# Attention of the first two batches: PE transposes in place of DMA transposes, small copies on GpSimd, key tiles with a pitch of 144

## The chip, the cores and the metric

One core of a Trainium2 chip runs the whole kernel. The metric is the device time of one execution in microseconds (us), taken as the median of several runs. TensorE is called PE, VectorE DVE, ScalarE ACT, GpSimd POOL or GpSimd, SyncE SP. SP issues DMAs only; ACT and GpSimd issue a few as well.

## The reference

Attention with RMS-normed queries and keys, followed by an MLP with a hard-swish-like activation. All inputs are float32.

```
q, k, v: (B=8, H=12, S=448, D=64);  g_q, g_k: (64,)
q_n = q / sqrt(mean(q*q, -1) + 1e-6) * g_q          # k_n the same with g_k
attn = softmax(q_n @ k_n.T / sqrt(64));  x = attn @ v
x -> (B*S = 3584, H*D = 768)
h = x @ w_in (768, 2048);  g = h * clip(h + 3, 0, 6) / 6;  out = g @ w_out (2048, 768)
```

## The kernel before

Heads go in pairs: a pair P is two heads of one batch, six pairs to a batch, 48 in all. A head has 448 rows; the first 384 ("main", three tiles of 128) are handled per pair, the last 64 ("rest") per two batches, so that two batches fill 128 partitions.

For a pair, q and k are loaded into `qk` (L145), squared (L136 on ACT for pairs under 4, L138 on GpSimd for the others), summed by DVE (L166), turned into 1/rms by ACT (L130, L131), and scaled to bf16 in `qks` by GpSimd (L178). v is cast into `va` by GpSimd (L188), which also builds `vbd`, the rest's v masked by head (L215). A DMA transpose issued by SP (`trans_pair`, L257) brings `qks` into `kq`, where keys and queries lie with the head dimension on the partitions. `pad_pair` then has DVE copy the 64 rest columns of q from `rT` into `kq` (L266) and write the keys twice into `kp`, each time multiplied by a column of `gmask` that is zero for one head of the two and holds the gains for the other (L269). The rest's q and k go the same way for two batches at once: scaled into `qkrs` (L233), transposed by DMA into `rT` (`trans_rest`, L240), padded into `kbd` by DVE (`pad_rest`, L248).

Scores are seven matmuls a pair into PSUM, 128 keys by 448 queries (L285); ACT takes the exponential of each (L286). `av` multiplies them with v into `x_ps` (L294, L297); DVE divides (L311, L313) into `xn`, and a DMA transpose (`xtrans`, L349) puts it into `xT`. The x of the rest goes over `xr` and `xrT`, from where DVE copies it into `xT` (L358).

The MLP of batch G reads `xT`: `h_part` (matmul L369, ACT L374, DVE L376 into `gT`) and `y_part` (matmul L388, DVE L394, store). `h` of batch b-1 and `y` of batch b-2 are merged into the attention of batch b by estimated cost, so batch 0 has no MLP beside it and batch 1 has `h` alone. The weights are loaded by GpSimd's DMA queue, w_in with pairs 3 to 9, w_out with pairs 11 to 14.

PSUM has three banks for scores, one each for `x_ps` and `r_ps`, and three (`ps_M`) for h and y. Pools set how far loads run ahead: five `qk`, four `vf`, four `kq`, three `kp`. Before the main loop a prologue sets the order of all engines by hand. In the main loop the program's order binds SP and GpSimd alone; the framework orders PE, DVE and ACT by readiness. `att_items(P)` emits, in this order: loads of P+6, the rest's step, squares of P+4, `trans_pair` and `pad_pair` of P+2, scaling and cast of P+3, the scores of P+1 merged with the av of P, and `xtrans` of P one pair later.

## Time and profile before

| | |
|---|---|
| time, three runs | 532.46 us median (524.71 to 533.09) |
| the profiled execution | 534.13 us, span 532.4 us |
| PE, matmul | 438.5 us busy, 82% of the span |
| DVE | 285.9 us, 54% |
| ACT | 298.8 us, 56% |
| GpSimd | 214.0 us, 40% |
| granted PE clock, mean | 0.946 of full speed |
| bytes by DMA | 67.44 MB, 127 GB/s over the span |

Busy shares are means over a span with different stages. The clock is a share of 2.4 GHz, of which 1.2 GHz is the lower level. The profiled execution is one run of its own; the rows below are of it.

### The profile page before, as it was taken

What the parts mean: (1) busy time and instruction counts of PE and PEld (TensorE: products, weight loads), DVE (VectorE), ACT (ScalarE), POOL (GpSimd) and SP (SyncE); (2) the same over time, 40 slices, a digit from 0 to 9 for tenths busy, and PEclk for the clock granted to TensorE, in tenths of its full rate; (3) what the DMA queues carried; (4) which work ended last, traced back from release to release, by engine and by line L of the source; (5) the groups of instructions that cost most, each with busy time, mean ns of one, the idle gap of its engine ahead of it and who ended that gap; (6) DMA issues with size and microseconds to landing.
All of it is one profiled execution on the core that took longest, in us unless ns stands there. A gap on an engine that the chain in (4) does not pass through costs nothing.

```text
span 532.4 us, 9016 instructions
## 1 busy us (share of the span) xinstructions
PE 438.5 (82%) x3344; PEld 254.0 (48%) x3344; DVE 285.9 (54%) x545; ACT 298.8 (56%) x583; POOL 214.0 (40%) x247
## 2 busy tenths in 40 slices
PE   0365565769988985999889997889978999999996
PEld 0143332436444553556444554555534566665553
DVE  2686476785645736555545636465545544334421
ACT  3665735757567754566566765576646766623310
POOL 3867676573534655154334643525234410000000
PEclk9987867888999999799998998999989999999999
DMA  9899999996658375435769365446664132120012
GB/s 207 214 224 191 196 140 216 187 186 142 147 140 165 85 185 112 96 96 144 142 139 145 90 170 127 98 98 154 161 109 83 45 90 60 31 76 30 15 64 70
DMA packets 139755, 67.44 MB, mean 127 GB/s; under 512 B 90560, under 2 KB 139712, under 8 KB 139712
## 3 DMA queue, kind: packets, MB, share of 16 engines
q1 hardware_dynamic: 131904, 59.99, 51.2%
q0 software_dynamic: 5440, 6.29, 8.0%
q10 hardware_dynamic: 2368, 0.59, 0.6%
q8 instruction: 26, 0.43, 0.3%
q14 instruction: 17, 0.14, 0.1%
HBM read 45.61 MB, written 11.01 MB: 106 GB/s over the span
## 4 chain that ended last, share of the span: by engine, by line
PE 45%; DMA 18%; issue 12%; DVE 11%; POOL 8%; SPq 3%; ACT 1%; POOLq 0%
PE y_ps L388 20%; PE h_ps L369 14%; DMA kq<-qks 10%; PE s_ps L285 6%; DVE kp L269 4%; PE x_ps L294 3%; POOL sq L138 3%; DMA qkr<-in_q_dram 3%; POOL qks L178 3%; DMA rT<-qkrs 2%; DMA qk<-in_q_dram 2%; DVE xn L313 1%; SPq L145 1%; DVE kq L266 1%; DVE kbd L248 1%
## 5 line engine op out<-in xcount | busy, mean ns | idle before, releaser
L286 ACT ACTIVATE eT<-s_ps,zero_c 128x448 bf16<-128x448 f32 x336 | 202.7, 634 | 79.7 <-PE s_ps L285 78.8
L369 PE MATMUL h_ps<-xT,w_in_sb 128*128 128x384 bf16 (+1 forms) x768 | 190.4, 364 | 20.3 <-DVE gT L376 12.9
L388 PE MATMUL y_ps<-w_out_sb,gT 128*128 128x384 bf16 x896 | 177.7, 331 | 12.9 <-DVE gT L376 12.6
L285 PE MATMUL s_ps<-kq,kp 128*128 128x448 bf16 x288 | 109.1, 387 | 30.6 <-DVE kp L269 30.0
L388 PEld LDWEIGHTS <-gT 128*128 128x128 bf16 x896 | 86.0, 99 | 68.9 <-issue 17.6
L374 ACT ACTIVATE t_sb<-h_ps,half_c 128x384 f32<-128x384 f32 (+1 forms) x128 | 80.9, 632 | 57.0 <-PE h_ps L369 36.9
L369 PEld LDWEIGHTS <-w_in_sb 128*128 128x128 bf16 x768 | 73.7, 100 | 73.2 <-issue 21.9
L188 POOL CAST va<-vf 128x384 bf16<-128x384 f32 x48 | 24.5, 509 | 194.3 <-PE r_ps L297 96.1
L376 DVE SCALAR_TENSOR_TENSOR gT<-t_sb,h_ps 128x384 bf16<-128x384 f32 (+1 forms) x128 | 78.6, 615 | 42.3 <-ACT t_sb L374 41.8
L294 PEld LDWEIGHTS <-eT 128*128 128x128 bf16 x1152 | 68.4, 105 | 65.5 <-issue 31.0
L269 DVE TENSOR_SCALAR kp<-kq,gmask 128x384 bf16<-128x384 bf16 x96 | 57.2, 626 | 78.0 <-DMA kq<-qks 77.9
L178 POOL TENSOR_TENSOR qks<-qk,rs 128x384 bf16<-128x384 f32 x96 | 77.8, 831 | 19.1 <-ACT rs L131 11.9
L294 PE MATMUL x_ps<-va,eT 128*128 128x65 bf16 x864 | 59.4, 203 | 24.8 <-DVE xn L313 20.2
L138 POOL TENSOR_TENSOR sq<-qk 128x768 f32<-128x768 f32 x44 | 64.6, 1468 | 5.8 <-DMA qk<-in_q_dram 5.7
L166 DVE TENSOR_REDUCE ssq<-sq 128x12 f32<-128x768 f32 x48 | 45.4, 946 | 32.5 <-POOL sq L138 24.8
L285 PEld LDWEIGHTS <-kp 128*128 128x128 bf16 x288 | 29.6, 104 | 59.5 <-DVE kp L269 35.2
L394 DVE COPY y_sb<-y_ps 128x384 f32<-128x384 f32 x56 | 31.0, 553 | 45.8 <-PE y_ps L388 45.7
L130 ACT ACTIVATE rs<-ssq,eps_c 128x12 f32<-128x12 f32 x48 | 14.6, 304 | 54.9 <-DVE ssq L166 54.9
L297 PE MATMUL x_ps<-vbd,eT 128*128 128x130 bf16 x144 | 33.6, 233 | 0.4
L313 DVE TENSOR_TENSOR xn<-x_ps,rd 128x384 bf16<-128x384 f32 x48 | 26.6, 554 | 1.2
L266 DVE COPY kq<-rT 128x64 bf16<-128x64 bf16 x48 | 23.3, 486 | 1.3 <-DMA rT<-qkrs 1.2
L294 PE MATMUL r_ps<-va,eT 128*128 128x65 bf16 x288 | 22.3, 201 | 0.1
(37 smaller groups left out, 175.4 us busy)
## 6 DMA issues: line engine op xcount, KB each, us to landing
qk<-in_k_dram SPq DMA_DIRECT2D x48, 192.0 KB, 2.9
qk<-in_q_dram SPq DMA_DIRECT2D x48, 192.0 KB, 2.9
vf<-in_v_dram SPq DMA_DIRECT2D x48, 192.0 KB, 3.6
out_dram<-y_sb SPq DMA_DIRECT2D x48, 192.0 KB, 2.1
w_in_sb<-in_moe_w_in_dram POOLq DMA_DIRECT2D x4, 768.0 KB, 9.8
w_out_sb<-in_moe_w_out_dram POOLq DMA_DIRECT2D x8, 384.0 KB, 6.2
qkr<-in_k_dram SPq DMA_DIRECT2D x8, 192.0 KB, 4.6
out_dram<-y_sb SPq DMA_DIRECT2D x16, 96.0 KB, 2.2
```

The lines of the kernel that those rows point to most:

```text
L138: nc.gpsimd.tensor_tensor(out=out, in0=x, in1=x, op=A_MULT)
L166: nc.vector.tensor_reduce(out=ssq[:], in_=sq[:].rearrange("p (n d) -> p n d", d=D), axis=AX_X, op=A_ADD)
L178: nc.gpsimd.tensor_tensor(out=qks[:, i].rearrange("p t h d -> p h t d"), in0=qk[:, i].rearrange("p h (t d) -> p h t d", d=D), in1=rs4[:, i ...
L269: nc.vector.tensor_scalar_mul(kp[:, a, :], kq[:, 0:SM], gmask[:, a:a + 1])
L285: nc.tensor.matmul(out=ps[:], lhsT=lhsT, rhs=st["qT", P], start=True, stop=True)
L286: nc.scalar.activation(out=st["e", P][:, u, :], in_=ps[:], func=EXP, bias=zero_c[:], scale=1.0)
L294: nc.tensor.matmul(out=dst[:, a * E1:(a + 1) * E1], lhsT=eT[:, u, c0:c0 + 128], rhs=va[:, a, t, :], start=(first and a == 0 and t == 0), s ...
L297: nc.tensor.matmul(out=dst, lhsT=eT[:, 2 * NT, c0:c0 + 128], rhs=vbd[:, j, :], start=False, stop=True, skip_group_check=True)
L369: nc.tensor.matmul(out=h_ps[:, 0:n], lhsT=w_in_sb[:, kt, f * 128:(f + 1) * 128], rhs=st["xT", G][:, kt, :], start=(kt == 0), stop=(kt == N ...
L374: nc.scalar.activation(out=t_sb[:, 0:n], in_=h_ps[:, 0:n], func=RELU, bias=half_c[:], scale=1.0 / 6.0)
L376: nc.vector.scalar_tensor_tensor(out=st["gT", G][:, f, :], in0=t_sb[:, 0:n], scalar=1.0, in1=h_ps[:, 0:n], op0=A_MIN, op1=A_MULT)
L388: nc.tensor.matmul(out=y_ps, lhsT=gT[:, f, i * 128:(i + 1) * 128], rhs=w_out_sb[:, f, nh * HALF:(nh + 1) * HALF], start=(f == 0), stop=(f ...
```

## The change

The transposes of the main part for pairs 0 to 11 (batches 0 and 1), of the rest of batches 0 and 1, and of x for pairs 0 to 11 are done by PE as matmuls with an identity, into the PSUM banks `ps_M`, from where DVE copies them out. The later ones stay DMA transposes. For pairs 0 to 11 the pad of the keys reads PSUM. The copy of the rest's q (`pad_pair`) and the pad of the rest's keys (`pad_rest`) go from DVE to GpSimd. The pad of a pair's keys is done in `trans_pair`, into a `kp` whose rows of 128 lie 144 elements apart. The squares of pairs 2 and 3 go from ACT to GpSimd, the mask of v's rest of batch 0 from GpSimd to ACT. The prologue's order is changed to suit.

```
@@ -4,6 +4,7 @@
 import concourse.bass as bass
 import concourse.tile as tile
 from concourse import bass_utils, mybir
+from concourse.masks import make_identity
 from concourse._compat import with_exitstack
 
 FP32 = mybir.dt.float32
@@ -45,12 +46,15 @@
     E1 = D + 1
     E2 = 2 * E1
     HALF = DM // 2
+    KPW = 144
     assert SR == 64 and D == 64 and NKT == NPAIR and B % 2 == 0
 
     pool = lambda name, bufs, **kw: ctx.enter_context(tc.tile_pool(name=name, bufs=bufs, **kw))
     const = pool("const", 1)
 
 
+    identity = const.tile([128, 128], BF16, name="identity")
+    make_identity(nc, identity[:])
     gq_t = const.tile([128, 1], FP32, name="gq_t")
     gk_t = const.tile([128, 1], FP32, name="gk_t")
     for a in range(2):
@@ -161,7 +165,7 @@
     def norm_pair(P):
         qk = st["qk", P]
         sq = sq_pool.tile([128, 4 * NT * D], FP32, name="sq", tag="sq")
-        square(sq[:], qk[:].rearrange("p a h x -> p (a h x)"), P < 4)
+        square(sq[:], qk[:].rearrange("p a h x -> p (a h x)"), P < 2)
         ssq = st_pool.tile([128, 4 * NT], FP32, name="ssq", tag="ssq")
         nc.vector.tensor_reduce(
             out=ssq[:], in_=sq[:].rearrange("p (n d) -> p n d", d=D), axis=AX_X, op=A_ADD)
@@ -212,8 +216,11 @@
     def prep_vrest(b, a):
         vr = st["vr", b]
         vbd = vbd_ring[b % NVB]
-        nc.gpsimd.tensor_scalar(
-            vbd[:, :, a * E1:a * E1 + D], vr[:], mask[:, a:a + 1], None, A_MULT)
+        dst = vbd[:, :, a * E1:a * E1 + D]
+        if b == 0:
+            nc.scalar.mul(dst, vr[:], mask[:, a:a + 1])
+        else:
+            nc.gpsimd.tensor_scalar(dst, vr[:], mask[:, a:a + 1], None, A_MULT)
         st["vbd", b] = vbd
 
     def norm_rest(b, i):
@@ -237,38 +244,58 @@
     def trans_rest(b):
         qks = st.pop(("qkrs", b))
         rT = rT_pool.tile([128, 2, NPAIR, 128], BF16, name="rT")
-        nc.sync.dma_start_transpose(
-            out=rT[:].rearrange("p a j c -> p (a j) c"), in_=qks[:].rearrange("p a h d -> p (a h d)"))
         st["rT", b // 2] = rT
+        if b >= 2:
+            nc.sync.dma_start_transpose(
+                out=rT[:].rearrange("p a j c -> p (a j) c"),
+                in_=qks[:].rearrange("p a h d -> p (a h d)"))
+            return
+        for i in (1, 0):
+            ps = ps_M.tile([128, NPAIR, 128], BF16, name="tr_ps", tag="M")
+            for j in range(NPAIR):
+                nc.tensor.transpose(
+                    ps[:, j, :], qks[:, i, 2 * j:2 * j + 2, :].rearrange("p h d -> p (h d)"),
+                    identity[:])
+            nc.vector.tensor_copy(out=rT[:, i], in_=ps[:])
 
     def pad_rest(b):
         e = b % 2
         kbd = kbd_pool.tile([128, NPAIR, 128], BF16, name="kbd")
         for a in range(2):
-            nc.vector.tensor_scalar_mul(
+            nc.gpsimd.tensor_scalar(
                 kbd[:, :, a * 64:(a + 1) * 64], st["rT", b // 2][:, 0, :, e * 64:(e + 1) * 64],
-                gmask[:, a:a + 1])
+                gmask[:, a:a + 1], None, A_MULT)
         st["kbd", b] = kbd
 
 
     def trans_pair(P):
         qks = st.pop(("qks", P))
         kq = kq_pool.tile([128, SM + S], BF16, name="kq")
-        nc.sync.dma_start_transpose(
-            out=kq[:, 0:2 * SM].rearrange("p (t c) -> p t c", c=128),
-            in_=qks[:].rearrange("p a t h d -> p (a t h d)"))
+        kp = kp_pool.tile([128, 2, NT, KPW], BF16, name="kp")
         st["kq", P] = kq
+        st["kp", P] = kp
+        if P >= 2 * NPAIR:
+            nc.sync.dma_start_transpose(
+                out=kq[:, 0:2 * SM].rearrange("p (t c) -> p t c", c=128),
+                in_=qks[:].rearrange("p a t h d -> p (a t h d)"))
+            keys = kq[:, 0:SM].rearrange("p (t c) -> p t c", c=128)
+        else:
+            ps = ps_M.tile([128, 2, NT, 128], BF16, name="t_ps", tag="M")
+            for i in (1, 0):
+                for t in range(NT):
+                    nc.tensor.transpose(
+                        ps[:, i, t, :], qks[:, i, t].rearrange("p h d -> p (h d)"), identity[:])
+            nc.vector.tensor_copy(
+                out=kq[:, SM:2 * SM], in_=ps[:, 1].rearrange("p t c -> p (t c)"))
+            keys = ps[:, 0]
+        for a in range(2):
+            nc.vector.tensor_scalar_mul(kp[:, a, :, 0:128], keys, gmask[:, a:a + 1])
 
     def pad_pair(P):
         b, j = divmod(P, NPAIR)
-        kq = st.pop(("kq", P))
         e = (b % 2) * 64
-        nc.vector.tensor_copy(out=kq[:, 2 * SM:], in_=st["rT", b // 2][:, 1, j, e:e + 64])
-        kp = kp_pool.tile([128, 2, SM], BF16, name="kp")
-        for a in range(2):
-            nc.vector.tensor_scalar_mul(kp[:, a, :], kq[:, 0:SM], gmask[:, a:a + 1])
-        st["qT", P] = kq[:, SM:]
-        st["kp", P] = kp
+        nc.gpsimd.tensor_copy(
+            out=st["kq", P][:, 2 * SM:], in_=st["rT", b // 2][:, 1, j, e:e + 64])
 
     UNITS = [(a, t) for t in range(NT) for a in range(2)]
 
@@ -278,11 +305,11 @@
             st["e", P] = e_pool.tile([128, NU, S], BF16, name="eT")
         if u < 2 * NT:
             a, t = UNITS[u]
-            lhsT = st["kp", P][:, a, t * 128:(t + 1) * 128]
+            lhsT = st["kp", P][:, a, t, 0:128]
         else:
             lhsT = st["kbd", b][:, j, :]
         ps = ps_S.tile([128, S], FP32, name="s_ps")
-        nc.tensor.matmul(out=ps[:], lhsT=lhsT, rhs=st["qT", P], start=True, stop=True)
+        nc.tensor.matmul(out=ps[:], lhsT=lhsT, rhs=st["kq", P][:, SM:], start=True, stop=True)
         nc.scalar.activation(out=st["e", P][:, u, :], in_=ps[:], func=EXP, bias=zero_c[:], scale=1.0)
 
     def av_group(P, dst, c0, first):
@@ -346,9 +373,16 @@
     def xtrans(P):
         b, j = divmod(P, NPAIR)
         xn = st.pop(("xn", P))
-        nc.sync.dma_start_transpose(
-            out=xT_of(b)[:, j, 0:SM].rearrange("p (t c) -> p t c", t=NT),
-            in_=xn[:].rearrange("p t a d -> p (t a d)"))
+        dst = xT_of(b)[:, j, 0:SM]
+        if P >= 2 * NPAIR:
+            nc.sync.dma_start_transpose(
+                out=dst.rearrange("p (t c) -> p t c", t=NT),
+                in_=xn[:].rearrange("p t a d -> p (t a d)"))
+            return
+        ps = ps_M.tile([128, NT, 128], BF16, name="xt_ps", tag="M")
+        for t in range(NT):
+            nc.tensor.transpose(ps[:, t, :], xn[:, t].rearrange("p a d -> p (a d)"), identity[:])
+        nc.vector.tensor_copy(out=dst, in_=ps[:].rearrange("p t c -> p (t c)"))
 
     def xtrans_rest(b, j0):
         xr = st["xr", b // 2]
@@ -539,29 +573,29 @@
         norm_rest(0, 1)
         rstd_rest(0, 0)
         rstd_rest(0, 1)
+        make_gmask()
         prep_qk(0)
         prep_rest(0, 0)
         prep_rest(0, 1)
         trans_pair(0)
+        norm_step(1)
         trans_rest(0)
-        norm_step(1)
+        pad_pair(0)
+        load_pair(3)
+        for a in range(2):
+            prep_vrest(0, a)
         prep_v(0)
         prep_pair(1)
-        load_pair(3)
-        trans_pair(1)
-        make_gmask()
-        norm_step(2)
-        pad_pair(0)
         pad_rest(0)
         for u in range(NU - 1):
             score(0, u)
-        prep_vrest(0, 0)
-        prep_vrest(0, 1)
+        norm_step(2)
         load_pair(4)
-        norm_step(3)
+        trans_pair(1)
         pad_pair(1)
         score(0, NU - 1)
         prep_pair(2)
+        norm_step(3)
         load_pair(5)
 
     with tc.manual_schedule(engines={mybir.EngineType.SP, mybir.EngineType.Pool}):
```

`make_identity` fills a 128 by 128 bf16 tile by two GpSimd operations.

## Rows read from the trace of the kernel before

**Rows 1.** Windows: start:end, length, busy us by engine, clock, DMA share, GB/s.

```profile
20.00:117.00 97.00, 61.22 (x474) 34.72 (x473) 68.38 (x101) 60.65 (x128) 64.65 (x72) 0.81 1.08 198
117.00:467.50 350.50, 316.42 (x2515) 185.77 (x2516) 187.91 (x391) 218.51 (x423) 138.81 (x150) 0.97 0.53 118
```

**Rows 2.** Line L286 up to 116.7 us: durations, first and last start.

```profile
L286 ACT ACTIVATE eT<-s_ps,zero_c x84: 614/634/697, 20.0 to 116.1; 128x448 bf16<-128x448 f32 x84
```

**Rows 3.** Chain of waits, 20 to 117 us: shares; one piece (start, us).

```profile
by line: DVE kp L269 14.7%; DMA qkr<-in_q_dram 10.3%; DMA kq<-qks 10.2%; PE s_ps L285 8.7%; DMA qk<-in_q_dram 8.6%; DVE kq L266 6.6%; PE h_ps L369 5.3%; DVE kbd L248 4.2%; PE x_ps L294 4.1%; DVE ssq L166 3.9%; DVE xn L313 3.4%; ACT eT L286 
...
54.51 10.03 DMA qkr<-in_q_dram
```

**Rows 4.** Timeline, DVE and GpSimd, 28 to 34 us: start, us, engine, line, operation.

```profile
28.38 5.43 DVE L266 COPY kq<-rT 128x64 bf16<-128x64 bf16 x1
...
28.84 1.49 POOL L138 TENSOR_TENSOR sq<-qk 128x768 f32<-128x768 f32 x1
...
30.27 1.62 POOL L178 TENSOR_TENSOR qks<-qk,rs 128x384 bf16<-128x384 f32 x2
...
32.30 1.46 POOL L138 TENSOR_TENSOR sq<-qk 128x768 f32<-128x768 f32 x1
33.72 0.31 DVE L269 TENSOR_SCALAR kp<-kq,gmask 128x384 bf16<-128x384 bf16 x1
```

**Rows 5.** Three DVE lines, whole span: duration ns min/median/max.

```profile
L269 DVE TENSOR_SCALAR kp<-kq,gmask x96: 302/321/3730, 18.9 to 444.9; 128x384 bf16<-128x384 bf16 x96
...
L358 DVE COPY xT<-xrT x8: 346/353/353, 106.0 to 474.2; 128x384 bf16<-128x384 bf16 x8
...
L394 DVE COPY y_sb<-y_ps x56: 540/557/559, 129.2 to 527.9; 128x384 f32<-128x384 f32 x56
```

**Rows 6.** Timeline from 105 to 107 us, one GpSimd and one DVE operation.

```profile
105.67 0.51 POOL L188 CAST va<-vf 128x384 bf16<-128x384 f32 x1 [2.51 <-PE r_ps L297]
...
105.96 0.35 DVE L358 COPY xT<-xrT 128x384 bf16<-128x384 bf16 x1 [1.44 <-DMA xrT<-xr]
```

**Rows 7.** Groups by line and form, DVE, 117 to 467.5 us.

```profile
L269 DVE TENSOR_SCALAR kp<-kq,gmask 128x384 bf16<-128x384 bf16 x70 | 34.0, 513 | 72.0 <-DMA kq<-qks 71.9
...
L266 DVE COPY kq<-rT 128x64 bf16<-128x64 bf16 x33 | 9.3, 280 | 0.1
```

**Rows 8.** Groups by line and form, 20 to 117 us: busy us, mean ns.

```profile
L269 DVE TENSOR_SCALAR kp<-kq,gmask 128x384 bf16<-128x384 bf16 x25 | 24.4, 1009 | 8.5 <-DMA kq<-qks 8.5
...
L266 DVE COPY kq<-rT 128x64 bf16<-128x64 bf16 x14 | 13.5, 966 | 0.0
...
L188 POOL CAST va<-vf 128x384 bf16<-128x384 f32 x13 | 6.6, 510 | 11.8 <-PE r_ps L297 5.5 <-PE x_ps L294 3.2 <-PE r_ps L294 3.1
L248 DVE TENSOR_SCALAR kbd<-rT,gmask 128x384 bf16<-128x384 bf16 x8 | 6.6, 846 | 0.0
L215 POOL TENSOR_SCALAR vbd<-vr,mask 128x384 bf16<-128x384 f32 x5 | 6.3, 1270 | 0.1
```

**Rows 9.** Windows, from 20 us to the end of pair 12's scaling.

```profile
20.00:93.90 73.90, 43.58 (x331) 24.21 (x331) 51.58 (x71) 44.44 (x94) 50.30 (x55) 0.78 1.07 201
```

**Rows 10.** Two matmuls: timeline at 28.48 us; L297 over the span.

```profile
28.48 0.54 PE L294 MATMUL x_ps<-va,eT 128*128 128x65 bf16 x6
...
L297 PE MATMUL x_ps<-vbd,eT x144: 217/218/315, 28.0 to 469.3; 128*128 128x130 bf16 x144
```

**Rows 11.** Timeline, 12 to 20 us: one SP issue, the first score.

```profile
15.07 1.42 SPq L240 DMA_TRANSPOSE rT<-qkrs  x1
...
19.45 1.09 PE L285 MATMUL s_ps<-kq,kp 128*128 128x448 bf16 x2 [19.45 <-DVE kp L269]
```

**Rows 12.** Waits of PE, 117 to 467 us: us in total, times, longest.

```profile
PE y_ps L388 <- DVE gT L376: 12.6, 6, 5.4
PE h_ps L369 <- DVE gT L376: 10.2, 6, 2.9
```

**Rows 13.** Waits of GpSimd, 20 to 117 us.

```profile
POOL qks L178 <- ACT rs L131: 10.8, 4, 4.3
```

## The prediction

> **What bounds the kernel now.** I read the busy time of the engines in stretches first, because the mean over the span (PE 82%) mixes two regimes. From 20 to 117 us no compute engine is near full (DVE leads with 68.4 of 97 us, PE has 61.2 at a granted clock of 0.81), while the DMA share is 1.08; from 117 to 467.5 us PE is busy 316.4 of 350.5 us at clock 0.97 [rows 1]. The border is no accident: the 84th exponential, the last one of pair 11, starts at 116.1 us [rows 2], so the first stretch is batches 0 and 1 (8 us a pair), the second the steady state in which attention and MLP overlap and PE sets the pace. What the change gives in the first stretch is therefore kept to the end, since everything behind it is a PE-bound train that starts earlier.
>
> What holds the first stretch is read from the chain of waits restricted to it [rows 3]. Two families own more than half. DVE's small SBUF operations (kp 14.7%, kq 6.6%, kbd 4.2%) have 25.5%, some 25 us. DMAs have another 29%: the transposes kq<-qks 10.2%, and loads of q (8.6% and 10.3%) that come late, one of them 10 us long. The timeline says why the DVE pieces are long [rows 4]: a copy of 64 columns starts at 28.38 and takes 5.43 us; GpSimd starts its square at 28.84 and runs one operation behind the other until 33.76; the copy ends at 33.81, and the next kp, with GpSimd quiet, takes 0.31 us. DVE is locked out while GpSimd has a queue of work. kp shows the same as a distribution: 302 ns at least, 3730 ns at most [rows 5].
>
> **The change, part by part.** *Wider pitch of kp.* With rows of 144 the output of the pad is three runs of 128 while its input stays one run of 384. One operation of the trace has this shape, the copy xT<-xrT: 346 to 353 ns in all eight, never longer [rows 5], and the first of them lies beside a GpSimd cast that began before it and ended after it [rows 6]. So I price a kp at 0.35 us from SBUF, and at 0.35 to 0.56 us from PSUM (the upper end is the y_sb copy of 384 columns from PSUM [rows 5]); I take 0.45. The Trainium skill's page VectorE: DVE Perf Modes, section What auto-detection actually checks, says that a copy or scalar operation takes its two-port mode only where the outermost counts of input and output are both even or equal; 384 against 3 is neither, which agrees with the 353 ns. Whether a scalar multiply follows the copy no row here shows; if it did not, the 70 kp of the steady state would keep their 34.0 us [rows 7] in place of 24.5.
>
> *DVE in the first stretch* [rows 8]: the 25 kp cost 24.4 us and would cost 25 x 0.45 = 11.3, so 13.1 go; the 14 kq copies (13.5 us) and 8 kbd pads (6.6 us) leave for GpSimd. Added are the evacuations of the PE transposes: per pair one of q and one of x (24 x 0.45 = 10.8 us), and two double ones for the rest of batch 0 (1.8 us). DVE falls by about 20.6, from 68.4 to some 48 us: no longer the engine that is late.
>
> *GpSimd* takes what DVE loses, and becomes the one to count. I count up to the end of pair 12's scaled q and k, at 93.9 us before; it had done 50.3 us of work from 20 us on [rows 9]. Added: 13 kq copies (64 columns; between 0.09 us, a sixth of the 384-column cast of 0.51 [rows 8], and that whole 0.51; I take 0.2, nearer the small end because the columns are a sixth and a fixed part stays) 2.6 us; kbd of batches 0 and 1, 4 x 1.27 = 5.1 us by the vbd multiply of the same size (2.0 by the cast; I take the multiply, the same operation with a scalar per partition) [rows 8]; the squares of pairs 2 and 3, 2 x 1.47 [rows 4] = 2.9 us; and the pair-1 scaling with two va casts, 2.6 us (1.62 [rows 4] and 2 x 0.51), which were over before 20 us and now wait behind the first q-rest copy. vbd of batch 0 goes to ACT, worth 0.5 us here. Together 50.3 + 2.6 + 5.1 + 2.9 + 2.6 - 0.5 = 63.0 us. ACT gains two small multiplies and loses two squares: nothing, ACT has 36 us idle in the stretch [rows 1].
>
> *PE* gets 12 x 9 + 12 = 120 transposes of 128 columns. In the trace six 65-column matmuls take 0.54 us together at this stage's clock, 0.09 each, and a lone 130-column one 0.217 to 0.315 us [rows 10]. I take 0.1 (they come in runs): 12 us on 61.2, within 97; the upper end, 38 us, is a rival. They wait in PE's queue for GpSimd's scaled q and k, and scores, x and h matmuls behind them wait too. The banks they write are those of h and y, which batch 0 does not use and batch 1 uses for h alone.
>
> *SP and DMA.* 25 transposes leave SP's queue and the DMA engines (12 kq, 12 x, 1 rest). SP no longer stops at xT for a DVE result with loads queued behind it, so the late loads of the chain [rows 3] should start earlier; I give them no gain of their own, since GpSimd, which consumes them, is already counted.
>
> *Start.* Before, the rest's DMA transpose is issued at 15.07 us and the first score starts at 19.45 [rows 11]. After: six transposes of the rest's q (0.6 to 1.2 us), a double evacuation (0.9), a GpSimd copy (0.2): some 17.0. That is 2.5 us, and the first exponential comes at 17.5. Building the identity puts two GpSimd operations ahead of the loads of g; gmask is wanted only with the first kp, hence nothing.
>
> *Sum of the first stretch.* GpSimd's 63.0 us would be the longest queue. How densely can it run? The busiest engine of this stretch manages 68.4/97 = 0.70 now, PE in the steady state 0.90 [rows 1]. I take 0.8, between them, because GpSimd still waits for the round trip square, sum, rstd. 63.0/0.8 = 79 us, plus 3 us from pair 12's scaling to its first exponential (six transposes, q and two kp), from 17.5: 99.3 us in place of 116.7. Gain 17.4; with 0.70 it is 6, with 0.90 it is 26.
>
> *Steady state.* PE is idle 34 us there, of which 22.8 wait for gT on DVE [rows 12]. DVE is relieved of the locks, 34.0 - 70 x 0.302 = 12.9 us in kp, pays 70 x 0.05 = 3.5 us back, and drops 9.3 us of kq copies [rows 7]: 19 of 188 us. Most of it is off the path; the waits for a kp whose DMA transpose is late stay as they are. I take 5 us, between 0 and 12 (half of the gT waits). GpSimd, busy 138.8 of 350.5 us [rows 1], has room for the copies and pads. The weight loads that GpSimd issues shift with its queue; w_in is wanted only from batch 1 on, w_out from batch 2.
>
> Profiled execution: 534.1 - 17.4 - 5 = 511.7 us. Its time stands at 534.1 against a median of 532.5, so times 0.997: 510 us.
>
> **The rivals.** *GpSimd packs no denser than now.* It is 64.65/97 = 0.67 busy today [rows 1], and its waits for rs are 10.8 us in this stretch, up to 4.3 at once [rows 13]. At 0.667 the stretch ends at 17.5 + 94.5 + 3 = 115, a gain of 2; with the 5 of the steady state 527, scaled 526. For it: every added operation is on this one in-order queue, and kbd now waits there for the rest's DMA transpose in even batches with squares and scaling queued behind. Against it: pair 12's scaling was ready 23 us before its exponential, so GpSimd was hardly ever the late one.
>
> *Transposes as dear as lone matmuls.* 120 x 0.315 = 38 us, 61.2 + 38 = 99 us of PE work in 97 us: no gain in the stretch, 529, scaled 527. Against it: they are six or three in a row. The Trainium skill's TensorE: Matmul & The Clock Gate, Part 4: PE-mode transpose, points this way: about 275 ns each inside a kernel, and a transpose does not count towards the full clock; as an estimate 33 us.
>
> *Slower: PE stands at the transposes.* If PE reaches them a GpSimd round trip too early, it stops with ready av and h work behind it, for each of pairs 2 to 11. At the longest wait of GpSimd for rs, 4.3 us [rows 13], that is 43 us: 534.1 - 22.4 + 43 = 555, scaled 553. It decides from 2.2 us a pair on. Against it: PE's order is by readiness, and only a wrong guess of GpSimd's pace does this.
>
> *More than forecast.* Density 0.9 and 12 us in the steady state: 534.1 - 26 - 12 = 496, scaled 494.
>
> **How the numbers follow.** Forecast 0.59, more than forecast 0.15, GpSimd as sparse as now 0.14, dear transposes 0.05, PE standing 0.07. A measurement of this kernel tells about 2%, some 10.6 us, from no change: faster means below 521.8. The first two cases give 0.75 of that (some of the forecast's spread falls short), the sparse and dear ones no change, 0.17, and standing slower, 0.08. The range runs from 492, just past the greater gain, to 527, the two cases without change.
>
> **What would show it.** Pair 12's first exponential near 99 us; no kp, kq or kbd above 0.6 us on DVE and no kq or kbd there at all; kp near 0.35 us from pair 12 on; GpSimd the busiest engine between 17 and 99 us, at some 0.8; transposes about 0.1 us apart; the first score near 17 us. Wrong would be the prediction if GpSimd ran at 0.67 or with waits for PE, if PE's idle time lay ahead of transposes, or if the steady stretch took longer than 350 us.

## The result and the profile after

The changed kernel takes 508.53 us (median of four runs, 507.30 to 512.61) where the kernel before takes 532.47 us (four runs, 524.71 to 533.09): a ratio of 0.961, 95% interval 0.949 to 0.973. A second measurement, told below, gave 0.962. The forecast was 510. Some executions of a kernel are over 1.5% longer than its fastest one; the ratios leave them out, and where the traced execution of a kernel below was such a one, its stretches are not read.

The profiled execution of the changed kernel took 512.61 us, the longest of its four, with a span of 510.8 us. Its stretches are cut at the same events as before: first exponential, first exponential of pair 12 (the 85th), end of the last. The windows view (start:end, length, busy us of PE, PEld, DVE, ACT, POOL, clock, DMA share, GB/s):

```profile
19.10:103.10 84.00, 60.77 (x569) 37.42 (x567) 44.10 (x100) 60.22 (x129) 77.72 (x95) 0.90 0.95 184
103.10:445.40 342.30, 315.96 (x2520) 186.31 (x2520) 171.55 (x352) 218.72 (x423) 156.25 (x194) 0.97 0.53 120
445.40:510.80 65.40, 60.41 (x361) 33.44 (x357) 21.59 (x37) 11.57 (x17) 0.00 (x0) 1.00 0.17 50
```

Against [rows 1], the first stretch is 84.0 us in place of 97, DVE does 44.1 us in it in place of 68.4, GpSimd 77.7 in place of 64.7. GpSimd is now busy 93% of the stretch; the next, PE, 72%. The steady stretch is 342.3 us in place of 350.5, and PE is as busy in it as before. The tail is the same 65 us. So of the 21.6 us of span, 0.9 lie ahead of the first exponential, some 12.8 in batches 0 and 1, 8.3 in the steady state.

The line of the exponentials answers to [rows 2] (its 84th starts 13.7 us earlier), and the chain of waits over the first stretch to [rows 3] (shares of the stretch):

```profile
L313 ACT ACTIVATE eT<-s_ps,zero_c x84: 613/633/668, 19.1 to 102.4; 128x448 bf16<-128x448 f32 x84
```

```profile
by line: POOL sq L142 19.7%; POOL qks L182 19.7%; issue 15.7%; DMA kq<-qks 9.5%; POOL kbd L265 6.1%; POOL va L192 6.1%; POOL vbd L223 3.9%; POOL qkrs L240 3.5%; POOL w_out_sb L558 3.3%; POOL w_in_sb L553 3.3%; POOL sqr L142 2.4%; POOL kq L2
```

The names that led before (kp, kq and kbd on DVE, late loads of q) are gone. All engines that the line names are GpSimd (it breaks off at kq); its squares and its scalings alone are 39% of the chain, and kbd, a new duty, is another 6%. The 15.7% called issue are time for which the profile shows no cause. The DMA transpose of a kq is still there because pairs from 12 on keep it.

The small operations, by line over the whole span (durations min/median/max in ns), in place of [rows 5]:

```profile
L292 DVE TENSOR_SCALAR kp<-kq,gmask x72: 370/405/415, 94.4 to 423.4; 128x384 bf16<-128x384 bf16 x72
L292 DVE TENSOR_SCALAR kp<-t_ps,gmask x24: 406/408/418, 15.6 to 85.2; 128x384 bf16<-128x384 bf16 x24
```

The spread is what to look at: no kp of 96 takes more than 418 ns, where the longest took 3730. But the shortest is 370, where it was 302. The groups of the first stretch (busy us, mean ns of one | idle before and its releaser) give the new prices beside those of [rows 8]:

```profile
L170 DVE TENSOR_REDUCE ssq<-sq 128x12 f32<-128x768 f32 x14 | 13.3, 951 | 21.7 <-POOL sq L142 21.6
...
L265 POOL TENSOR_SCALAR kbd<-rT,gmask 128x384 bf16<-128x384 bf16 x6 | 7.4, 1236 | 2.0 <-DMA rT<-qkrs 2.0
...
L288 DVE COPY kq<-t_ps 128x384 bf16<-128x384 bf16 x11 | 3.9, 356 | 8.0 <-PE t_ps L286 6.6 <-PE r_ps L321 1.4
...
L297 POOL COPY kq<-rT 128x64 bf16<-128x64 bf16 x13 | 3.0, 231 | 0.0
```

The first of these rows holds the new bottleneck: DVE, which is no longer short of time, stands 21.6 us in front of its sum of squares until GpSimd has squared. Why that costs anything is seen in the timeline from 86 to 93 us (start, us, engine, line, operation, idle before and releaser):

```profile
85.93 0.33 PE L384 MATMUL xt_ps<-identity,xn 128*128 128x128 bf16 x3
...
86.25 2.46 POOL L265 TENSOR_SCALAR kbd<-rT,gmask 128x384 bf16<-128x384 bf16 x2 [2.05 <-DMA rT<-qkrs]
...
88.70 1.23 POOL L223 TENSOR_SCALAR vbd<-vr,mask 128x384 bf16<-128x384 f32 x1
89.91 1.46 POOL L142 TENSOR_TENSOR sq<-qk 128x768 f32<-128x768 f32 x1
...
91.40 0.95 DVE L170 TENSOR_REDUCE ssq<-sq 128x12 f32<-128x768 f32 x1 [5.37 <-POOL sq L142]
...
92.27 0.35 DVE L385 COPY xT<-xt_ps 128x384 bf16<-128x384 bf16 x1
...
92.67 1.12 PE L403 MATMUL h_ps<-xT,w_in_sb 128*128 128x384 bf16 x3 [4.63 <-DVE xT L385]
```

PE has transposed x at 86.3. Its evacuation is a 0.35 us copy on an idle DVE, but DVE takes its work in order and stands at the sum for a pair four ahead; that waits for a square, which stands on GpSimd behind two kbd pads and one vbd, and the pads themselves had waited 2.05 us for the rest's DMA transpose. When GpSimd is through, the copy runs at 92.27 and PE goes on at 92.67, after 4.63 us. The wait is put down to DVE's xT; its cause is GpSimd's queue, two steps back. The waits of PE over the first stretch (total us, times, longest) say the same in sum, and those of GpSimd answer to [rows 13]:

```profile
PE t_ps L286 <- POOL qks L182: 9.6, 7, 4.9
PE h_ps L403 <- DVE xT L385: 4.8, 2, 4.6
PE t_ps L286 <- DVE gT L410: 2.9, 1, 2.9
```

```profile
POOL qks L182 <- ACT rs L135: 2.2, 2, 1.6
POOL kbd L265 <- DMA rT<-qkrs: 2.0, 1, 2.0
```

PE now waits for GpSimd; GpSimd itself stands about 6 us of the 84 (it waited 10.8 us for rs alone before, 2.2 now).

The start, by the timeline, in place of [rows 11]:

```profile
14.29 0.82 PE L286 MATMUL t_ps<-identity,qks 128*128 128x128 bf16 x6 [14.29 <-POOL qks L182]
...
16.77 1.46 PE L256 MATMUL tr_ps<-identity,qkrs 128*128 128x128 bf16 x12 [1.66 <-POOL qkrs L240]
...
17.64 1.20 DVE L259 COPY rT<-tr_ps 128x768 bf16<-128x768 bf16 x2 [0.47 <-PE tr_ps L256]
...
18.25 0.24 POOL L297 COPY kq<-rT 128x64 bf16<-128x64 bf16 x1 [1.54 <-DVE rT L259]
...
18.54 1.28 PE L312 MATMUL s_ps<-kq,kp 128*128 128x448 bf16 x3 [0.31 <-POOL kq L297]
```

From the scaled rest (16.77) to the first score it is 1.8 us; before, from the issue of the rest's DMA transpose, 4.4 [rows 11].

In the steady state PE's waits for gT, in place of [rows 12], are 19.1 us instead of 22.8. Its whole idle time there fell by 7.8 us, from 34.1 to 26.3; its waits for xn (7.3 before, 4.9 now) and for y_sb (3.3 and 2.1) are most of the rest.

```profile
PE h_ps L403 <- DVE gT L410: 10.1, 5, 3.9
PE y_ps L422 <- DVE gT L410: 9.0, 5, 3.6
```

### The profile page after: what moved, and what is told of

Its sections match the earlier page's. It is cut to its first block, busy times and chain, and to the rows that moved or that the text cites. A ratio compares the mean times of both kernels' runs of the same rounds, so it can differ in the third digit from the quotient of the medians.

```text
span 510.8 us, 9231 instructions
## 1 busy us (share of the span) xinstructions
PE 440.0 (86%) x3464; PEld 259.3 (51%) x3464; DVE 244.5 (48%) x507; ACT 298.2 (58%) x583; POOL 241.7 (47%) x313
## 4 chain that ended last, share of the span: by engine, by line
PE 61%; DMA 13%; POOL 13%; issue 4%; DVE 4%; SPq 2%; ACT 1%; POOLq 0%; DVEq 0%; ACTq 0%
PE y_ps L422 26%; PE h_ps L403 22%; DMA kq<-qks 12%; PE s_ps L312 7%; POOL sq L142 4%; PE x_ps L321 3%; POOL qks L182 3%; POOL kbd L265 1%; PE r_ps L321 1%; DMA qk<-in_k_dram 1%; PE x_ps L324 1%; DVE gT L410 1%; POOL va L192 1%; DVE kp L292 1%; POOL qkrs L240 1%
## 5 line engine op out<-in xcount | busy, mean ns | idle before, releaser
L312 PE MATMUL s_ps<-kq,kp 128*128 128x448 bf16 x288 | 105.5, 376 | 3.0 <-DVE kp L292 2.3
L321 PEld LDWEIGHTS <-eT 128*128 128x128 bf16 x1152 | 65.5, 102 | 39.5 <-DVE xn L340 8.1
L142 POOL TENSOR_TENSOR sq<-qk 128x768 f32<-128x768 f32 x46 | 67.4, 1466 | 0.1
L292 DVE TENSOR_SCALAR kp<-kq,gmask 128x384 bf16<-128x384 bf16 x72 | 27.3, 406 | 80.6 <-DMA kq<-qks 80.4
L321 PE MATMUL x_ps<-va,eT 128*128 128x65 bf16 x864 | 54.9, 198 | 5.1 <-DVE xn L340 4.9
L324 PE MATMUL x_ps<-vbd,eT 128*128 128x130 bf16 x144 | 32.4, 225 | 0.3
L286 PE MATMUL t_ps<-identity,qks 128*128 128x128 bf16 x72 | 7.5, 250 | 26.8 <-POOL qks L182 23.9
L340 DVE TENSOR_TENSOR xn<-x_ps,rd 128x384 bf16<-128x384 f32 x48 | 26.7, 555 | 1.2
L286 PEld LDWEIGHTS <-qks 128*128 128x128 bf16 x72 | 5.3, 111 | 31.3 <-POOL qks L182 27.6
```

Of the source, the lines that this page charges most:

```text
L142: nc.gpsimd.tensor_tensor(out=out, in0=x, in1=x, op=A_MULT)
L292: nc.vector.tensor_scalar_mul(kp[:, a, :, 0:128], keys, gmask[:, a:a + 1])
L312: nc.tensor.matmul(out=ps[:], lhsT=lhsT, rhs=st["kq", P][:, SM:], start=True, stop=True)
L321: nc.tensor.matmul(out=dst[:, a * E1:(a + 1) * E1], lhsT=eT[:, u, c0:c0 + 128], rhs=va[:, a, t, :], start=(first and a == 0 and t == 0), s ...
L324: nc.tensor.matmul(out=dst, lhsT=eT[:, 2 * NT, c0:c0 + 128], rhs=vbd[:, j, :], start=False, stop=True, skip_group_check=True)
```

## The experiments

Theory after the result: the PE transposes bring the gain by taking the DMA round trip off the path from scaled keys to scores; after that GpSimd's queue sets the pace of batches 0 and 1. Rivals: the gain is the lifted lock of DVE (copies and pitch); PE, or the transposes on it, sets the pace; the loads freed in SP's queue do it.

The kernels ran in three groups. Times are medians of all executions; a ratio is between means, to the kernel before in the same group (its median was 531.02 us in the group of the first four kernels, 526.74 in that of the second four, 531.19 in that of the last three). Where groups are compared, ratios are. Each kernel is the changed one with the edit shown and keeps the rest of the change; the new order of the prologue was not undone by itself. Of "GpSimd's squares twice" and "kbd on VectorE" only the times are read. The stretches of the others, cut at the same exponentials in one traced execution of each (us):

| kernel | time | ratio, 95% | first exponential | first stretch | steady | tail |
|---|---|---|---|---|---|---|
| before (profiled run 534.13) | 532.47 | 1 | 20.0 | 96.8 | 350.6 | 64.9 |
| changed (profiled run 512.61) | 508.53 | 0.961 (0.949 to 0.973) | 19.1 | 84.0 | 342.2 | 65.4 |
| changed, measured again | 508.80 | 0.962 (0.956 to 0.968) | 17.8 | 82.9 | 340.9 | 65.4 |
| PE transposes alone | 513.27 | 0.973 (0.963 to 0.983) | 19.1 | 86.8 | 346.5 | 65.0 |
| copies and pitch alone | 527.20 | 0.996 (0.992 to 1.001) | 20.2 | 104.0 | 336.1 | 64.9 |
| pitch of 128 | 514.20 | 0.971 (0.962 to 0.980) | 18.6 | 84.2 | 345.5 | 65.4 |
| early pads on ScalarE | 502.63 | 0.952 (0.942 to 0.962) | 18.7 | 76.9 | 340.3 | 65.0 |
| GpSimd's squares twice | 520.12 | 0.983 (0.974 to 0.991) | | | | |
| transposes twice | 514.61 | 0.974 (0.966 to 0.981) | 18.2 | 85.8 | 345.8 | 65.4 |
| kbd on VectorE | 503.63 | 0.952 (0.944 to 0.960) | | | | |
| two squares more on ScalarE | 507.33 | 0.962 (0.954 to 0.969) | 19.2 | 77.0 | 343.6 | 65.0 |
| ScalarE early, VectorE late | 506.45 | 0.958 (0.951 to 0.965) | 19.4 | 75.4 | 344.8 | 65.0 |
| x by DMA | 516.89 | 0.976 (0.969 to 0.983) | 18.7 | 85.1 | 346.2 | 65.1 |

**PE transposes alone.** Copies and pads back on DVE, pitch 128.

```diff
-    KPW = 144
+    KPW = 128
-        nc.gpsimd.tensor_copy(out=st["kq", P][:, 2 * SM:], ...
+        nc.vector.tensor_copy(out=st["kq", P][:, 2 * SM:], ...
-            nc.gpsimd.tensor_scalar(kbd[...], ..., gmask[:, a:a + 1], None, A_MULT)
+            nc.vector.tensor_scalar_mul(kbd[...], ..., gmask[:, a:a + 1])
```

> The changed kernel with the q-rest copy and the kbd pad back on DVE and the pitch of kp back at 128; the PE transposes stay. My theory, that locks and DMA transposes each held part of batches 0 and 1: DVE's small operations show blocked times over 1 us again, some 20 to 30 us in batches 0 and 1, pair 12 starts 5 to 10 us later than in the changed kernel, time about 518. Rival A, the transposes alone made the gain: 507 to 511. Rival B, the locks alone made it: 526 to 533.

513.27 us, between my 518 and rival A: without the copies and the pitch most of the gain is left (0.973 against 0.961). The locks are back, as the timeline of DVE and of GpSimd at 51 us shows:

```profile
51.10 5.31 DVE L297 COPY kq<-rT 128x64 bf16<-128x64 bf16 x1
51.15 5.26 DVE L288 COPY kq<-t_ps 128x384 bf16<-128x384 bf16 x1
51.42 4.99 DVE L340 TENSOR_TENSOR xn<-x_ps,rd 128x384 bf16<-128x384 f32 x1
51.89 4.53 DVE L292 TENSOR_SCALAR kp<-t_ps,gmask 128x384 bf16<-128x384 bf16 x2
```

```profile
51.67 1.26 POOL L223 TENSOR_SCALAR vbd<-vr,mask 128x384 bf16<-128x384 f32 x1
52.89 1.47 POOL L142 TENSOR_TENSOR sq<-qk 128x768 f32<-128x768 f32 x1
54.31 1.61 POOL L182 TENSOR_TENSOR qks<-qk,rs 128x384 bf16<-128x384 f32 x2
55.88 0.50 POOL L192 CAST va<-vf 128x384 bf16<-128x384 f32 x1
```

A copy of 64 columns is held for 5.31 us while GpSimd runs one operation behind the other, and the records of the DVE operations behind it, which read PSUM, all end with it at 56.41. So the durations of locked neighbours overlap, and a kp from PSUM with 4530 ns need not have been locked itself: with the same pitch of 128 and no locked copy ahead of it ("pitch of 128", below), none of 24 takes more than 418 ns. Yet in this kernel the first stretch is only 2.8 to 3.9 us longer than with the whole change. DVE is busy, locked time counted in, 71.3 us of its 86.8, GpSimd 66.4 where it was 77.7: the locks are back on DVE, GpSimd is rid of 11 us, and the two nearly cancel. In this stretch the moved copies put one long queue in place of another, for a gain of 3 to 4 us.

**Copies and pitch alone.** All transposes by DMA again.

```diff
-        if P >= 2 * NPAIR:      (keys and queries; x)
+        if P >= 0:
-        if b >= 2:              (rest)
+        if b >= 0:
```

> The changed kernel with all transposes by DMA as before; the copies stay on GpSimd and the pitch at 144. My theory: the chain of batches 0 and 1 holds DMA transposes again (some 10 us of kq and loads that queue behind them), time about 519. Rival A, the transposes alone: 530 to 534. Rival B, the locks alone: 507 to 511.

527.20 us, 0.996: no measurable gain, far from my 519 and nearest to rival A. DVE is free of locks (no kp above 415 ns in the whole span), but the first stretch is longer than before, 104.0 us. DVE's longest wait, and the head of the kernel's chain, from 20 to 124 us:

```profile
DVE kp L292 <- DMA kq<-qks: 40.8, 8, 12.7
```

```profile
by line: DMA kq<-qks 28.5%; DMA qk<-in_q_dram 11.8%; issue 10.6%; POOL qks L182 6.1%; PE h_ps L403 5.2%; POOL sq L142 3.2%; ACT eT L313 3.1%; POOL va L192 2.9%; SPq L378 2.6%; DMA qk<-in_k_dram 2.5%; DVE kp L292 2.5%; SPq L149 2.0%; PE s_ps
```

What the lock had cost was handed on to the DMA transpose of the keys: 28.5% of the chain in place of 10.2% [rows 3], 40.8 us of DVE's waits in place of 8.5 [rows 8]. GpSimd stands too: its new copies and pads wait for the rest's DMA transpose, 3.7 us at the start and 5.1 us at 95 us, with scalings and squares behind them. Relief of the engine that leads the busy shares gives nothing while the transpose stays on the path. Parts of 0.973 and 0.996 do not quite make up 0.961, which would fit copies that are worth more once the DMA transposes are gone; the intervals leave that undecided.

**Pitch of 128.** Only the pitch undone.

```diff
-    KPW = 144
+    KPW = 128
```

> The changed kernel with kp rows 128 apart, nothing else. My theory: kp from SBUF (pairs 12 on) goes back to about 0.31 us when GpSimd rests and over 1 us when it does not, 10 to 13 us blocked in all, mostly off the path: 510 to 514. Rival, the pitch is worth the whole gain of the steady state (8 us): 516. Rival, it is worth nothing: 507 to 509, with kp never blocked.

514.20 us, 0.971: the pitch seems worth some 5 us, though the intervals overlap (0.962 to 0.980; 0.956 to 0.968 for the changed kernel measured again). The stretches put it into the steady state (345.5 against 342.2 and 340.9), where kp reads SBUF. The line of these kp:

```profile
L292 DVE TENSOR_SCALAR kp<-kq,gmask x72: 273/319/3153, 93.9 to 426.1; 128x384 bf16<-128x384 bf16 x72
```

The median is 0.09 us below that of the wide pitch, but the mean of the 70 in the steady stretch is 440 ns against 406. The sum of that, 2.4 us, is less than the gain. One lock makes the difference of the means (400 ns without it): the kp of 3153 ns starts at 102.3 us, at the border of the two stretches, and the next longest has 1414. Behind it on DVE stands an xn, for which PE waits 3.7 us; in the two traces of the changed kernel PE's wait for xn about there is 1.4 and 0.7 us. Over the steady stretch PE waits 9.6 us for xn, against 4.9 and 5.4. What that lock cost lies in the work behind it on DVE.

**Early pads on ScalarE.** GpSimd relieved of six kbd and four vbd pads.

```diff
+            if b < 3:
+                nc.scalar.mul(kbd[...], ..., gmask[:, a:a + 1])
+            else:
                 nc.gpsimd.tensor_scalar(kbd[...], ..., gmask[:, a:a + 1], None, A_MULT)
-        if b == 0:   (vbd)
+        if b < 3:
```

> The changed kernel with the kbd pads and the vbd masks of batches 0 to 2 on ACT. My theory, GpSimd bounds batches 0 and 1: it sheds 2 x 1.24 us a batch of kbd and as much of vbd, some 9 us before pair 12, and pair 12 starts 5 to 8 us earlier: 500 to 504. Rival, PE and ACT bound batch 1 (pair 12's scaled q and k lay 21 us ahead of its exponential): 507 to 510, or later by ACT's 6 to 8 us of added work.

502.63 us, 0.952, with "kbd on VectorE" the lowest ratio here; its interval just overlaps that of the changed kernel, but the first stretch, 76.9 us against 84.0 and 82.9, says where the gain lies. The windows:

```profile
18.70:95.60 76.90, 57.81 (x572) 36.75 (x572) 45.62 (x103) 62.56 (x138) 65.18 (x85) 0.91 0.99 203
95.60:435.80 340.20, 311.67 (x2519) 184.05 (x2517) 170.56 (x350) 218.01 (x424) 155.80 (x193) 0.98 0.53 120
```

12.5 us less of GpSimd work shorten the first stretch by 6 to 7 us, and GpSimd falls to 85% busy; then it begins to wait for PE (6.8 us of va behind av matmuls). Its queue was the bound, and is one among several now.

**GpSimd's squares twice**, for pairs 4 to 11: eight more squares, 11.8 us by the 1.47 of one.

```diff
             nc.gpsimd.tensor_tensor(out=out, in0=x, in1=x, op=A_MULT)
+            if twice:
+                nc.gpsimd.tensor_tensor(out=out, in0=x, in1=x, op=A_MULT)
-        square(..., P < 2)
+        square(..., P < 2, 4 <= P < 12)      (the last argument is twice)
```

> The changed kernel with the GpSimd square of pairs 4 to 11 computed twice into the same tile: 8 x 1.47 = 11.8 us more of GpSimd in batches 0 and 1, nothing else, and the same output. My theory, GpSimd bounds that stretch, through the sum of squares that DVE waits for: pair 12 starts 8 to 12 us later, time 517 to 521. Rival, PE and ACT bound it: at most 3 us, 508 to 512.

520.12 us, 0.983 against 0.962: 2.1% or some 11 us, nearly all of what was added, and the intervals do not touch (0.974 to 0.991; 0.956 to 0.968). Added GpSimd time costs about one for one, relieved time gives half. Together with "early pads on ScalarE" this shows that GpSimd's queue paces batches 0 and 1.

**Transposes twice.** Each of the 108 PE transposes of batches 0 and 1 for pairs (keys, queries, x) issued two times.

```diff
-                for t in range(NT):
+                for t in [t for t in range(NT) for _ in range(2)]:
```

> The changed kernel with each PE transpose of a pair (of q and k, and of x) issued twice into the same place: 108 transposes more, the same output. My theory, transposes cost PE 0.06 to 0.1 us each and PE has slack: plus 0 to 4 us, 508 to 513. Rival, they cost what a lone matmul takes, 0.22 to 0.31 us, or PE bounds the stretch: plus 15 us or more, above 520.

514.61 us, 0.974 against 0.962: some 6 us, more than my 0 to 4 and far less than the rival's 15; the intervals overlap. The price of a transpose is better read from the first stretch. PE is busy with transposes of pairs for 17.5 us there, 10.6 in the changed kernel: 7 us for 96 more, 0.07 each, far from the 0.22 to 0.31 us of a lone matmul [rows 10]. The stretch is only 2 to 3 us longer, with PE busy 61.9 of 85.8 us; PE's waits for scaled keys shrink from 9.6 to 2.9 us. The other 4 to 5 us of the 6 lie in the steady state, where hardly anything is doubled. Those I can't place.

**kbd on VectorE**, with the wide pitch kept.

```diff
-            nc.gpsimd.tensor_scalar(kbd[...], ..., gmask[:, a:a + 1], None, A_MULT)
+            nc.vector.tensor_scalar_mul(kbd[...], ..., gmask[:, a:a + 1])
```

> The changed kernel with the kbd pad alone back on DVE, the pitch stays. The pad can be locked out again (0.3 to over 2 us each), GpSimd sheds 2.5 us a batch. My theory: GpSimd's relief of 5 us before pair 12 outweighs the locks of four pads, 503 to 507. Rival, the locks are what the move was for: 510 to 515.

503.63 us, 0.952 against 0.962, as my theory had it. The two intervals overlap a little (0.944 to 0.960 and 0.956 to 0.968); the likeliest reading is that moving kbd to GpSimd cost the change some 5 us, which fits 7.4 us of kbd on the bounding queue.

**Two squares more on ScalarE**, added to "early pads on ScalarE".

```diff
-        square(..., P < 2)
+        square(..., P < 4)
```

> The kernel with the kbd pads and vbd masks of batches 0 to 2 on ACT, and besides the squares of pairs 2 and 3 on ACT again, as before the change (2.9 us less of GpSimd, 1.7 us more of ACT). My theory, GpSimd is still the bound of the first batches: 1 to 3 us below the kernel without the squares, 499 to 502. Rival, ACT and PE have taken over: 502 to 505.

507.33 us, 0.962: longer than either forecast, no better than the pads alone (0.952, intervals overlapping), and the first stretch is no shorter (77.0). GpSimd is down to 62.4 us of 77, but now DVE waits for the square on ACT (6.1 us, up to 5.1 at once), in whose queue the exponentials stand. Relief of GpSimd has an end here.

**The changed kernel again**, as anchor for the last group, with no edit.

> The changed kernel itself, so that the other kernels of this job can be compared with it on one chip. A ratio of about 0.96 to the kernel before, that is 507 to 512 us where the kernel before takes about 530. If it comes out at 0.97 or above here, the doubled transposes cost less than the 6 us that the ratios gave.

508.80 us, 0.962. The trace shows one thing more: the first exponential comes at 17.8 us, not 19.1. The first square starts at 8.52 us, as before the change (8.53), where in the first trace of the changed kernel it waited for its load until 9.91.

**ScalarE early, VectorE late.** Early pads on ScalarE, and kbd of batches 3 to 7 on VectorE.

```diff
             if b < 3:
                 nc.scalar.mul(kbd[...], ..., gmask[:, a:a + 1])
             else:
-                nc.gpsimd.tensor_scalar(kbd[...], ..., gmask[:, a:a + 1], None, A_MULT)
+                nc.vector.tensor_scalar_mul(kbd[...], ..., gmask[:, a:a + 1])
```

> Padded rest keys and rest values of batches 0 to 2 on ScalarE, and the padded rest keys of batches 3 to 7 on VectorE in place of GpSimd. Theory (GpSimd sets the pace of the first two batches, and GpSimd's long two-port operations hold nothing up later): the first two batches as with ScalarE's help alone (pair 12's first exponential at 95 to 97 us), and the steady state like that kernel's or a little shorter, 498 to 503 us. Rival (the helping engines are themselves near their bound, so that what one gains the other loses): no better than with either alone, 503 to 508 us.

506.45 us, 0.958: the rival's "no better than with either alone". The first stretch is the shortest of all, 75.4 us, but the steady one is 344.8, 4.5 us longer than with the early pads alone. PE waits there for gT on DVE for 23.8 us against 22.8, which is 1 us of these 4.5. In the steady state of that kernel GpSimd has room (busy 156 of 340 us) and DVE is what PE waits for, which would leave the late kbd on GpSimd; that this is better is not shown, since the intervals overlap (0.951 to 0.965; 0.942 to 0.962) and steady stretches differ by as much without a cause that I know.

**x by DMA.** Only the MLP's inputs transposed by DMA again.

```diff
         dst = xT_of(b)[:, j, 0:SM]
-        if P >= 2 * NPAIR:
+        if P >= 0:
```

> The MLP's inputs of batches 0 and 1 transposed by DMA as before; keys, queries and the rest by TensorE as in the changed kernel. Theory (the gain of the transposes lies in the chain from the scaled keys to the scores, and the MLP's input is a pair or more away from it): within 4 us of the changed kernel, either way. Rival (every DMA transpose taken from SP's queue counts, since it blocks the loads behind it, and the square of four pairs ahead waits for these loads): 5 to 12 us slower than the changed kernel, with GpSimd waiting for loads again in the first two batches.

516.89 us against 508.80 in the same group, with runs that do not overlap (514.09 to 518.28; 508.30 to 509.95): 8.1 us. My theory (within 4) falls. The rival's size is right, its mechanism isn't: GpSimd's waits of the first stretch name no load. They do name another transfer: the kbd pads stand 4.3 us for the rest's DMA transpose, against 1.7 in the anchor. 1.0 us of the loss lies ahead of the first exponential, 2.2 in the first stretch and 5.2 in the steady state, where PE is as busy as in the anchor (315.9 and 315.2 us) and idle 4.6 us longer. Part of that is a longer wait for gT (21.7 against 18.3 us); the rest stays open.

## Why the prediction was right, and where only its sum was

The total came out within 1.5 us, and the kind of mechanism is shown: first two batches shortened by leaving the DMA round trip, with the locks as a smaller part, everything behind starting earlier, GpSimd the engine that then bounds. That the sum fits so well is luck in part: pair 12's first exponential was forecast at 99.3 us and came at 103.1 (100.7 in the second trace), a gain of 13.7 and not 17.4, and the steady state gave 8.3 and not 5. Step by step:

- *kp, and the lock.* That the wide pitch takes kp out of the lock is shown twice, by a longest kp of 415 ns in 96 with the pitch of 144 and all transposes by DMA, and 3153 with the pitch of 128. It agrees with the Trainium skill's page VectorE: DVE Perf Modes, section What auto-detection actually checks, and settles that a scalar multiply follows a copy there. One reading that the prediction leaned on is wrong: the cast of [rows 6] ends at 106.18, 0.13 us before the copy beside it and not after it; they ran side by side for 0.22 us. The price was forecast at 0.35 us from SBUF and 0.45 from PSUM and is 0.405 and 0.408; the multiply is 52 ns dearer than the copy of its shape.
- *DVE in the first stretch.* 48 us forecast, 44.1 measured; the evacuations cost 0.35 us each (0.45 forecast). No longer late: right.
- *GpSimd's work.* 63.0 us forecast from 17.5 us to the end of pair 12's scaling; 61.7 measured. The kq copy is 0.23 us (0.2), kbd 1.24 (1.27).
- *Density: mis-sized.* The scaling of pair 12 ends at 82.3 us, so the 61.7 us ran in 64.8: 0.95, not 0.8. GpSimd's waits for rs, on which the 0.8 rested, fell from 10.8 to 2.2 us. The rival "GpSimd packs no denser than now" falls with it.
- *Lag: mis-sized, and it made up for the density.* From the end of pair 12's scaling to its first exponential I put 3 us, the work in between. It is 20.8 us (19.7 in the second trace). Before the change it had been 23 us, and I read these as slack, "GpSimd was hardly ever the late one". But the program has a pair scaled two steps ahead of its scores, and squared three: when the scaling of pair 12 ends, 68 exponentials have started, and those of pairs 10 and 11 are still to come. The lead is not fixed (10.3 us at pair 6, 11.9 at pair 9) and it is not slack: GpSimd is busy 16.9 of these 20.8 us, and the wait of PE in the timeline from 86 to 93 us lies in them. The stretch must be counted with all that GpSimd does until pair 12's first exponential, 77.7 us, not 63.0; with my 0.8 that is 97 us, as long as before the change. Two errors of 14 and 18 us cancelled: 79 + 3 = 82 us forecast from 17.5, 64.8 + 20.8 = 85.6 measured.
- *PE.* 0.1 us a transpose taken, 0.08 (six in 0.50 us at 83 us) to 0.14 (at the start) measured, and doubling them adds 0.07 of PE's time each. "As dear as lone matmuls" is out. The Trainium skill's TensorE: Matmul & The Clock Gate, Part 4: PE-mode transpose has about 275 ns each and no full clock; single records here have 216 to 314 ns, but they overlap in a run. The granted clock of the first stretch is 0.90 and 0.88 in the two traces with 120 transposes in the kernel, 0.81 before the change and 0.86 with all transposes by DMA; these stretches differ in more than the transposes, so what one does to the clock is not shown. "PE stands at the transposes" is partly so: 9.6 us of waits for scaled keys, 12.5 with a gT, not 43. By the sign that the prediction had set (PE's idle time lies ahead of transposes) this counts against it: it is more than half of PE's 23.2 idle us. But PE had been idle for 35.8 us of the stretch before.
- *Start.* First score forecast at 17.0 and first exponential at 17.5: 17.20 and 17.8 in the second trace, so the step is right. In the profiled run both come 1.3 us later; the first square had waited for its load. The identity delays nothing that these traces show.
- *SP and DMA given no gain.* Too little: x by DMA costs 8 us, though not by the late loads that I had named, as far as the waits show.
- *Steady state.* 5 us forecast (0 to 12), 8.3 measured, 9.7 in the second trace. The pitch would have 3 to 5 of it by the kernel without it, which is no more than the unexplained spread below. DVE's busy time fell by 16 us (19 forecast), and the waits for gT by 3.7.

Open stays the steady state of the single kernels, which ranges from 336 to 347 us without a full account by their edits: with transposes doubled and with x by DMA, edits of batches 0 and 1, it is 4 to 5 us longer than in the changed kernel. The shortest, 336.1 us with copies and pitch alone, is no gain by the edit: PE is idle in it as long as in the changed kernel (26.7 and 26.3 us) and busy 309.5 us in place of 316.0, at a granted clock of 0.99 in place of 0.97. Over the whole span that execution had 0.964, the nine others of the same kernel 0.937 to 0.946, at much the same time. Why the clock differed stays open.

## What to carry to other kernels

Find the queue that is late after the change and count all of its work in the stretch; a producer that ends its part of a pair 20 us before the consumer needs it is not early by that much if it has no idle time. Whether it paces is seen by adding to its work: here 11.8 us more cost about 11. A change that relieves the engine with the highest share may hand the whole gain to the next wait on the same chain (0.996 for the copies alone), so take the round trip off the path first. Work that is moved for a lock costs on the queue that receives it: put it on the engine that has room in that stretch, here ScalarE in batches 0 to 2.

## What I had not expected of the hardware

- A DVE copy waited 5.31 us through several GpSimd operations in a row; it was not let in between two of them. Records of DVE operations behind it, three of them reading PSUM, began beside it and ended with it.
- GpSimd's multiply of 384 bf16 columns by a scalar per partition takes 1.24 us, its cast of as many columns 0.50, its product of two tensors 0.82 (the scaling).
- With rows of 144 a kp costs 0.09 us more in the median than with 128, and 0.03 us less in the mean over the steady stretch, but the latter by a single lock of 3.15 us. What such a lock costs is the work behind it: PE waited 3.7 us.
